# First rows of q through ScalarE's DMA queue, first rows of k through SyncE's

## The chip, the core and the metric

The kernel runs on one core of one Trainium2 chip. The metric is device time in microseconds, the median of several executions. The engines are named as in the profile: PE (TensorE), DVE (VectorE), ACT (ScalarE), POOL (GpSimd) and SP (SyncE); PEld is TensorE's weight load. SP, ACT and POOL can each issue DMA transfers through a queue of their own.

## The reference

Sliding-window causal attention (window 64) over q, k and v of shape 8 x 8 x 576 x 64 (batch, heads, positions, head dimension), and then a soft mixture of 8 experts with 4 slots each on the 4608 rows of 512 that come out:

```
scores = (q @ k^T) / 8, kept where 0 <= i - j < 64
attn   = softmax(scores);   x = attn @ v  ->  [4608, 512]
logits = x @ phi                              # 32 slots
d      = softmax over rows(logits);  slot_input = d^T @ x
slot_out[e] = relu(slot_input[e] @ w1[e]) @ w2[e]    # 8 experts
c      = softmax over slots(logits);  out = c @ slot_out
```

All inputs and the output are fp32 in device memory.

## The kernel before

The attention works on 32 pairs of heads, p = 0 to 31, four for each batch element. The order of all instructions is written out by hand; the loop at L553 interleaves the stages of several pairs, so that each engine executes its own instructions in the order of the text and waits where an operand is not there.

The rows of q and k are loaded in groups of four heads ("a quad"), two pairs. One partition holds six consecutive positions of a head, so a group is a tile of 96 partitions x 4 heads x 384 elements. `load_k` and `load_q` (L79) load groups 1 to 15 through POOL's queue, and these transfers turn fp32 into fp16 on their way. Group 0 is loaded otherwise, at L100 to L107: as fp32, without a cast, by four transfers of two heads (one pair) each, all issued by SP (L103) in the order k pair 0, q pair 0, k pair 1, q pair 1. They are put into memory that later holds the weights w1 of experts 5 and 4, which is why the profile calls them `w`. Each is 288 KB. `round_rows` (L110) then turns each into fp16, in tiles `ks` and `qs`: k pair 0 on ACT, q pair 0 on DVE, k pair 1 on DVE, q pair 1 on ACT.

From there: TensorE transposes the rows (`st_transpose`, L316, into PSUM tiles a_k and a_q); ACT or DVE copies them into `kT` (`st_copy_k`, L327 or L324) and `qb` (`st_copy_q`, L336, the second half of the first pair on DVE, L333). `st_max` (L346, L349) computes scores for the row maxima, which DVE reads at L353; `st_score` and `st_exp` (L372 to L381) compute them again for the exponentials; `st_av` (L405) multiplies with v; DVE normalises (L415). The transposed result goes through the slots' logits and a running soft dispatch (the `fr_` functions).

On ACT the first instructions are the load of the activation table and the copy into `lh` (L211), a constant of the masks. On DVE, constants are set before the cast of q pair 0 (L230), and the masks `wm` are copied (L233) between that cast and the cast of k pair 1 (L235). Behind that one stands the DVE half of `qb` (L333). After the four transfers SP issues one of phi (L254, 64 KB).

POOL's queue loads, after group 0, all of q, k and v, and the weights w1 and w2 of the experts as buffers come free (`load_w` L133 and L135, `load_half` L150 and L155). After the attention the experts are computed: `first` (L816), `turn_hidden` (L831), `second` (L837) and `second_last` (L846), the last of which uses the two tiles `w2h` that are loaded last. `osb` (L904, L910) takes the slots' outputs, half the columns each. `give` (L882) multiplies them with the combine weights, ACT and DVE scale the result in turn (L899, L897), and SP issues the output (L901): 14 transfers, the first three of the first half of the columns, the rest behind the second half.

Of the kernel before, what the change touches and what calls it, by code (L numbers as in the profile page):

```python
# [18 lines left out]
def kernel(  # L19
# [10 lines left out]
    nc = tc.nc  # L30
# [37 lines left out]
    RP = S // RQ  # L68
# [31 lines left out]
    for i, (src, tag, pr) in enumerate(((k, "ks", 0), (q, "qs", 0), (k, "ks", 1), (q, "qs", 1))):  # L100
        f = w1_t[5 - i // 2, 0][:, :, :].rearrange("p c f -> p (c f)").bitcast(FP32)
        f = f[0:RP, 768 * (i % 2):768 * (i % 2) + 768].rearrange("p (h x) -> p h x", h=2)
        nc.sync.dma_start(out=f, in_=src[0].rearrange("h (p r) d -> p h (r d)", p=RP)[:, 2 * pr:2 * pr + 2, :])  # L103
        if pr == 0:
            staged[tag] = pin.tile([128, 4, RQ * Dh], FP16, name=tag, tag=tag)
        first_rows[tag, pr] = f
        staged[tag, pr] = staged[tag], 2 * pr  # L107
# [569 lines left out]
    b, p = B - 1, NP - 1  # L677
# [273 lines left out]
```

## Time and profile before

| | |
|---|---|
| median of 3 runs | 191.47 us (191.35 to 192.05) |
| the profiled execution | 191.22 us |
| its span | 189.4 us |
| TensorE busy | 160.4 us (85%) |
| VectorE busy | 142.9 us (75%) |
| ScalarE busy | 144.9 us (76%) |
| GpSimd busy | 98.5 us (52%) |
| moved by DMA | 41.47 MB, mean 219 GB/s |
| of it GpSimd's queue (q0, software_dynamic) | 30.35 MB |
| of it SyncE's (q1, hardware_dynamic) | 10.68 MB |

The profiled execution has its own time, 191.22 us: the span of the trace and 1.8 us around it. All rows of the profile belong to that execution. A DMA row tells the issue (on the issuing engine's own row, as SPq) and, in the DMA view, the time from issue to landing. The share of a queue is the time that its packets took, added up over 16 DMA engines, and is over 100% where packets of an engine overlap. MB are counted as written, so a transfer that turns fp32 into fp16 reads twice as many.

### The profile page before, as it was taken

Reading aid. Unit: us, or ns where it says so; the run is one execution under the profiler, and the core shown is the slowest. Engines: PE = TensorE matmul, PEld = TensorE weight load, DVE = VectorE, ACT = ScalarE, POOL = GpSimd, SP = SyncE. Lnnn points to the kernel's source line nnn. Section 1 sums busy time; section 2 is a strip of 40 time slices with the busy share of each in tenths; the row PEclk is TensorE's granted clock in tenths of the full one; section 3 lists DMA queues with packets and bytes.
Section 4 is the critical chain, followed back from the end, with each engine's and each line's share of the span. In section 5 each row is a group of like instructions: output and inputs, shape, how many; then the busy total and the mean of one; then the engine's idle time right before and its main releaser. Section 6 shows DMA issues by size and latency. Waiting matters only on the chain. (4 is left out here: it accounts for less than half of the span.)

```text
span 189.4 us, 7060 instructions
## 1 busy us (share of the span) xinstructions
PE 160.4 (85%) x3036; PEld 120.5 (64%) x3036; DVE 142.9 (75%) x352; ACT 144.9 (76%) x266; POOL 98.5 (52%) x123
## 2 busy tenths in 40 slices
PE   5787999999999999999999899999989897769500
PEld 1466878877777777777777787776774365633100
DVE  6798796897888889788878988888886555289800
ACT  6487879989889898988999898988588256379600
POOL 7857927273695554983984828727854160000000
PEclk9999999999999999999999999999999999999955
DMA  6999999999999999999999999999999999979996
GB/s 153 222 184 185 226 175 223 179 223 179 185 226 180 210 192 184 207 196 185 210 195 192 211 182 198 199 204 195 213 214 212 204 196 179 277 258 422 415 415 252
DMA packets 61630, 41.47 MB, mean 219 GB/s; under 512 B 38816, under 2 KB 57504, under 8 KB 60704
## 3 DMA queue, kind: packets, MB, share of 16 engines
q0 software_dynamic: 56560, 30.35, 116.1%
q1 hardware_dynamic: 5040, 10.68, 15.9%
q8 instruction: 23, 0.38, 0.7%
q14 instruction: 7, 0.06, 0.1%
HBM read 61.93 MB, written 9.44 MB: 377 GB/s over the span
## 5 line engine op out<-in xcount | busy, mean ns | idle before, releaser
L336 ACT ACTIVATE qb<-a_q 64x576 f16<-64x576 f16 x63 | 40.6, 645 | 5.5 <-PE a_q L316 4.0
L353 DVE TENSOR_REDUCE m<-a_m 128x8 f16<-128x1024 f32 x32 | 39.2, 1224 | 1.0
L381 ACT ACTIVATE pt<-a_s 128x1024 f16<-128x1024 f32 x32 | 32.8, 1024 | 6.6 <-PE a_s L375 5.4
L180 POOL COPY v<-v 64x1152 f16<-64x1152 f16 x16 | 18.3, 1142 | 32.8 <-DMA v<-in_v_dram 32.6
L415 DVE TENSOR_TENSOR x_b<-a_v,rc 128x640 f16<-128x640 f32 x31 | 25.6, 825 | 1.1
L349 PEld LDWEIGHTS <-qb 128*128 128x128 f16 x256 | 16.8, 98 | 7.8 <-ACT qb L336 0.4
L346 PE MATMUL a_m<-wm,ident_h 128*128 128x512 f16 x64 | 19.3, 384 | 0.9 <-DVE m L353 0.9
L375 PEld LDWEIGHTS <-lh 128*128 128x128 f16 x288 | 18.8, 98 | 1.9 <-issue 1.7
L173 POOL DMA_DIRECT2D v<-in_v_dram x16 | 19.8, 1235 | 0.0
L372 PEld LDWEIGHTS <-kT 128*128 128x128 f16 x288 | 18.6, 98 | 1.6 <-issue 1.4
L372 PE MATMUL a_s<-qb,kT 128*128 128x128 f16 x256 | 19.5, 219 | 0.0
L349 PE MATMUL a_m<-kT,qb 128*128 128x128 f16 x256 | 19.5, 219 | 0.0
L375 PE MATMUL a_s<-rt,lh 128*128 128x128 f16 x256 | 19.5, 219 | 0.0
L433 ACT COPY xt<-a_k 128x576 f16<-128x576 f16 x28 | 17.9, 640 | 2.0 <-PE a_k L429 0.7
L182 POOL COPY v<-v 64x1088 f16<-64x1088 f16 (+1 forms) x16 | 17.9, 1120 | 0.8
L405 PE MATMUL a_v<-v,pt 128*64 128x65 f16 x558 | 15.6, 196 | 2.1 <-DVE m L363 1.1
L897 DVE TENSOR_SCALAR w<-cp,rcs 128x512 f32<-128x512 f32 (+1 forms) x22 | 12.9, 635 | 5.7 <-PE cp L892 5.4
L367 DVE CAST rt<-a_v 9x128 f16<-9x128 f32 x30 | 8.7, 289 | 11.0 <-PE a_v L366 10.7
L327 ACT ACTIVATE kT<-a_k 128x576 f16<-128x576 f16 x24 | 15.7, 654 | 0.8 <-PE a_k L316 0.8
L405 PEld LDWEIGHTS <-pt 128*64 128x64 f16 x576 | 13.5, 110 | 4.3 <-DVE m L363 1.8
L79 POOL DMA_DIRECT2D ks<-in_k_dram x15 | 10.4, 696 | 10.9 <-PE a_s L375 3.0
L316 PE MATMUL a_q<-ident_h,qs 96*64 96x96 f16 x384 | 14.7, 206 | 1.6 <-DVE a_q L225 1.3
(182 smaller groups left out, 332.6 us busy)
## 6 DMA issues: line engine op xcount, KB each, us to landing
w<-in_moe_w_dram POOLq DMA_DIRECT2D x13, 1024.0 KB, 16.8
out_dram<-w SPq DMA_DIRECT2D x9, 768.0 KB, 6.2
v<-in_v_dram POOLq DMA_DIRECT2D x16, 288.0 KB, 12.4
ks<-in_k_dram POOLq DMA_DIRECT2D x15, 288.0 KB, 15.2
qs<-in_q_dram POOLq DMA_DIRECT2D x15, 288.0 KB, 12.5
out_dram<-w SPq DMA_DIRECT2D x2, 640.0 KB, 4.4
w1h<-in_moe_w_dram POOLq DMA_DIRECT2D x4, 256.0 KB, 15.9
w<-in_moe_w_dram POOLq DMA_DIRECT2D x4, 256.0 KB, 14.8
```

The lines of the kernel that those rows point to most:

```text
L173: nc.gpsimd.dma_start(out=v1s[b % 2][:, c, 0:Dh], in_=v[b].rearrange("h s d -> (h s) d").rearrange("(c p) d -> p c d", p=128)[:, c, :])
L180: nc.gpsimd.tensor_copy(out=v2[64:128, c0:c1, 0:Dh], in_=v1[0:64, c0:c1, 0:Dh])
L182: nc.gpsimd.tensor_copy(out=v2[0:64, c0:c1, 0:Dh], in_=v1[64:128, c0 - 1:c1 - 1, 0:Dh])
L336: nc.scalar.activation(qbs[p % NQ][h, :, hf, :], turned(a_qh)[h], AF.Copy, scale=QKS)
L346: nc.tensor.matmul(a_m[:, j, :], ident_h[:, :], wm[:, j:j + 4, :].rearrange("p c x -> p (c x)"), start=True, stop=False, skip_group_check= ...
L349: nc.tensor.matmul(a_m[:, i // 4, 128 * (i % 4):128 * (i % 4) + 128], qblock(p, i), kwindow(p, i), start=False, stop=True, skip_group_chec ...
L353: nc.vector.reduce_max(ms[p % 2][:, 64:72].rearrange("p (l c) -> p l c", l=2), a_m[:, :, :].rearrange("p l (c x) -> p l c x", x=128), axis ...
L372: nc.tensor.matmul(at(i), kwindow(p, i), qblock(p, i), start=(i % 4 == 0), stop=False, skip_group_check=True)
L375: nc.tensor.matmul(at(i), lh[:, i, :], rt[:, :], start=False, stop=True, skip_group_check=True)
L381: nc.scalar.activation(st_pt(p)[:, 0:8, :].rearrange("p i x -> p (i x)"), a_s[:, :, :], AF.Exp, scale=XS)
L405: nc.tensor.matmul(a_v[r0:r0 + 64, hf, 65 * (i // 2):65 * (i // 2) + 65], pt[:, i, 64 * hf:64 * hf + 64], rhs, start=True, stop=True, skip ...
L415: nc.vector.tensor_tensor(out=xbs[b][:, :, 128 * hp:128 * hp + 128].rearrange("p c (l d) -> p l c d", l=2), in0=avv[:, :, :, 0:64], in1=rc ...
```

## The change

The two transfers of q (pair 0 and pair 1) are issued by ScalarE, the two of k by SyncE as before. The sizes, the destinations and the order in the text stay; everything else is unchanged.

```
     for i, (src, tag, pr) in enumerate(((k, "ks", 0), (q, "qs", 0), (k, "ks", 1), (q, "qs", 1))):
         f = w1_t[5 - i // 2, 0][:, :, :].rearrange("p c f -> p (c f)").bitcast(FP32)
         f = f[0:RP, 768 * (i % 2):768 * (i % 2) + 768].rearrange("p (h x) -> p h x", h=2)
-        nc.sync.dma_start(out=f, in_=src[0].rearrange("h (p r) d -> p h (r d)", p=RP)[:, 2 * pr:2 * pr + 2, :])
+        eng = nc.sync if tag == "ks" else nc.scalar
+        eng.dma_start(out=f, in_=src[0].rearrange("h (p r) d -> p h (r d)", p=RP)[:, 2 * pr:2 * pr + 2, :])
         if pr == 0:
             staged[tag] = pin.tile([128, 4, RQ * Dh], FP16, name=tag, tag=tag)
```

In ScalarE's order the two issues stand ahead of the table load and the copy into `lh`. In SyncE's order the issues of k pair 1 and of phi move up by one and by two places. The orders of TensorE, VectorE and GpSimd are the same as before. Lines after L102 have numbers higher by one in the changed kernel.

More of the change, by code (lines that the diff above doesn't have):

```diff
@@ L102 @@
         f = f[0:RP, 768 * (i % 2):768 * (i % 2) + 768].rearrange("p (h x) -> p h x", h=2)
-        nc.sync.dma_start(out=f, in_=src[0].rearrange("h (p r) d -> p h (r d)", p=RP)[:, 2 * pr:2 * pr + 2, :])
+        eng = nc.sync if tag == "ks" else nc.scalar
+        eng.dma_start(out=f, in_=src[0].rearrange("h (p r) d -> p h (r d)", p=RP)[:, 2 * pr:2 * pr + 2, :])
         if pr == 0:
```

## The prediction

> **What bounds the kernel now.** I read the page first, then the order of time in the first 20 us, the landing of each early transfer, the waits, and the last loads. Two stretches matter: the start, where the change is, and 163 us, where the last weights arrive.
>
> The start, in the timeline (start us, duration us, engine, line, operation, idle before and its releaser):
>
> ```profile
> 0.73 1.28 ACT L211 ACT_TABLE_LOAD   x1 [0.73 <-PEq L935]
> 1.17 0.44 SPq L103 DMA_DIRECT2D w<-in_q_dram  x1
> 2.16 1.15 ACT L211 COPY lh<-db 64x1152 f16<-64x1152 f16 x1
> 4.15 0.83 ACT L110 CAST ks<-w 96x768 f16<-96x768 f32 x1 [0.85 <-DMA w<-in_k_dram]
> 5.57 0.56 DVE L110 CAST qs<-w 96x768 f16<-96x768 f32 x1 [1.32 <-DMA w<-in_q_dram]
> 6.04 0.96 DVE L233 COPY wm<-wb 64x640 f16<-64x640 f16 x2
> 7.11 0.86 DVE L110 CAST ks<-w 96x768 f16<-96x768 f32 x1
> 8.01 0.76 DVE L333 TENSOR_SCALAR qb<-a_q 64x576 f16<-64x576 f16 x1
> 8.79 0.83 ACT L110 CAST qs<-w 96x768 f16<-96x768 f32 x1 [1.48 <-DMA w<-in_q_dram]
> 8.85 0.61 PE L349 MATMUL a_m<-kT,qb 128*128 128x128 f16 x8
> ```
>
> Call the four transfers k0, q0, k1, q1. The path to the first score maxima (L349 at 8.85) is VectorE's: it waits 1.32 us for q0, then runs the q0 cast, the mask copies, the k1 cast and its half of qb (L333) almost without a gap. ScalarE's part, kT done at 6.42 and its half of qb at 7.31, is early by 1.4 us or more.
>
> Landing of the four, from windows around each issue (the last number is us from issue to landing):
>
> ```profile
> w<-in_k_dram SPq DMA_DIRECT2D x1, 288.0 KB, 3.4
> w<-in_q_dram SPq DMA_DIRECT2D x1, 288.0 KB, 4.4
> w<-in_k_dram SPq DMA_DIRECT2D x1, 288.0 KB, 5.4
> w<-in_q_dram SPq DMA_DIRECT2D x1, 288.0 KB, 6.6
> ```
>
> Issued at 0.74, 1.17, 1.65 and 2.15, they land at 4.14, 5.57, 7.05 and 8.75: one each 1.45 to 1.7 us, although the issues are 0.45 us apart. So the transfers, not SyncE's issues, set the pace; k1 lands 0.06 us before VectorE is ready for it.
>
> How fast they run, in two half-microsecond windows of the DMA view (the first line from 4.5 us, the other three from 6.5; q1 is SyncE's queue, q0 GpSimd's, with packets, MB and share of 16 engines):
>
> ```profile
> DMA packets 74, 0.11 MB, mean 221 GB/s; under 512 B 2, under 2 KB 74, under 8 KB 74
> DMA packets 129, 0.12 MB, mean 241 GB/s; under 512 B 15, under 2 KB 129, under 8 KB 129
> q0 software_dynamic: 72, 0.06, 70.5%
> q1 hardware_dynamic: 57, 0.07, 51.3%
> ```
>
> At 4.5 us the only queue at work is SyncE's, with 74 packets in half a microsecond and a share near 98%. At 6.5 us GpSimd's queue (72 packets) works beside it (57), and together they finish 129. GpSimd's packets read fp32 and write fp16, so they are not the same load, but a second queue seems to fill engine time that one alone leaves.
>
> The end of the loads, in the waits (total us, times, longest):
>
> ```profile
> POOL v L180 <- DMA v<-in_v_dram: 32.6, 11, 4.7
> PE op L846 <- DMA w2h<-in_moe_w_dram: 0.8, 1, 0.8
> ```
>
> GpSimd's queue moves 1.86 to 2.09 MB in each 10 us from 20 to 160 us, landings there are 12 to 19 us after issue, and GpSimd itself waits for DMA. That stream is never empty. Its last w2h, issued at about 153.3, lands near 163.55; TensorE, ready at 162.97, waits for it until 163.75. Every full-width output comes after that matmul (L846). So time won by the computing engines at the start is held again there, and time lost is free up to 0.78 us. Only an earlier end of the load stream moves the end by itself.
>
> The sum is made against the profiled execution: 191.22 us, span 189.4 and 1.8 around it, 0.25 below the median of 191.47; the difference is applied to the median. A measurement of this kernel can tell about 0.5% (0.96 us) from no change.
>
> **SyncE.** Two issues go (0.44 and 0.45). k1 is issued at 1.17 instead of 1.65, phi at 1.65 instead of 2.64. phi landed at 10.9 and is first used at 26.6, so 0. The first outputs are issued from 160.49: 0.
>
> **ScalarE.** It now issues q0 and q1 ahead of the table load. On SyncE such an issue took 0.38 to 0.45, so I take 0.89 for two; bounds 0 (hidden beside the load) and 2.5 (two of GpSimd's longest, 1.26). Queued behind: the table load 1.62 to 2.90, the lh copy 2.90 to 4.05, then the k0 cast, which waited for DMA until 4.15. The 0.85 us of that wait just covers it. At 2.5 the cast begins at 5.7, kT ends at 8.0 and ScalarE's qb at 8.6, still ahead of L333's end at 8.77. So 0, as long as VectorE's chain stays where it is.
>
> **The transfers.** q0 is issued 0.44 earlier and q1 0.97, and each now runs beside a k transfer. Cost from both sides:
> - No overlap: both of a pair end when the second did, so k0 and q0 at about 5.57, k1 and q1 at about 8.6. k0 is covered. k1 is not: VectorE casts it at 8.6 instead of 7.11, L333 stands behind it, and TensorE's L349 behind that: +1.49.
> - Full overlap: 129 packets against 74 to 80, say 1.68 times the pace, so a pair takes 2.90/1.68 = 1.73. Counting 1.45 back from k0's landing gives 2.69 for a common origin: k0 and q0 at 4.42, k1 and q1 at 6.15. Then VectorE casts q0 at 4.42 to 4.98, copies the masks until about 6.05, casts k1 at 6.15 to 7.0 and ends L333 at about 7.8; L349 begins at 7.85, 1.0 earlier. The next k group, on GpSimd's queue, lands at 9.55 (issue 2.05 + 7.5; used at 10.21), and the next q group at 11.4 (2.88 + 8.5; used at 12.25), which caps the gain at 0.85.
>
> I take the second, as the window with two queues lies nearer to it: -0.85 for the computing engines. [...]
>
> **The load stream.** From 5 to 7 us SyncE's queue holds 95.5, 96.3, 81.7 and 51.3% of the engines by half microseconds, 1.62 us in all, while GpSimd's stream only begins (0.09 MB in 2 us, against 0.20 MB per us later). With full overlap the pairs are through at about 5.6, which leaves 1.0 us of engine time to the stream. Its first packets come at about 5.2 and rise slowly, so I take half: w2h 0.5 earlier. Against it, first outputs 0.85 earlier (57% of the engines' time from 160 to 165 was theirs) take from w2h's last packets, up to 0.4; I take 0.2. Net -0.3, bounds -1.0 and +0.4.
>
> Sum: TensorE ready at 162.1, w2h at 163.25, so the end moves by -0.3; 190.9 against the profiled execution, 191.2 as a median.
>
> **The rivals.**
> - *Pairs share the engines, no overlap.* One mechanism: k1 lands at 8.6 and VectorE's in-order queue holds L333 behind its cast. For it: the single queue's share is already 92 to 113%. Against it: 129 packets at 6.5 us. L349 +1.49, less the 0.78 that TensorE waits for w2h: +0.7, 192.2. It decides once k1 lands after 7.11 + 0.78 = 7.9. Bounds 0 (TensorE was only 81% busy from 10 to 20 us and may catch up) and +1.49 (192.95). [...]
> - *The stream moves with the start.* If GpSimd's first packets were held up by SyncE's, all of the 1.0 us comes back: w2h at 162.55, TensorE ready at 162.1, so -1.0, 190.5; bounds -0.8 and -1.5. Against it: the stream rose slowly, as if still being written.
> - *Nothing changes in kind.* The two queues are served one after the other, landings stay within 0.3 us: 191.5.
>
> **How the numbers follow.** Forecast 0.50, own range 190.6 to 191.9; pairs sharing 0.28; stream moving 0.17; nothing 0.05. Faster by over 0.5% (below 190.51): 0.13 of the stream case and 0.04 of the forecast's lower end, 0.17. Slower (above 192.43): 0.12 of the sharing case's upper part and 0.01 of the forecast, 0.13. The rest, 0.70, is within 0.5%. The range goes from 190.3 to 192.3.
>
> **What would show it.** Right: q0 lands at about 4.4 and k1 at about 6.2, L349 begins near 8.0, TensorE's wait for w2h at L846 grows from 0.78 to about 1.3, and GpSimd's queue has more than 0.09 MB by 7 us. Sharing is shown by k1 landing after 7.9, L349 after 9.6 and no wait at L846. The stream case shows in w2h landing by 162.7. The forecast is wrong if w2h lands where it did and the end still moves, or if ScalarE's two issues take so long that the k0 cast begins after 5.7.

## The result, and the profile after

| | before | changed kernel |
|---|---|---|
| median of 22 runs | 191.75 us (191.35 to 192.79) | 193.54 us (191.36 to 197.86) |
| the profiled execution, its span | 191.22, 189.4 us | 193.58, 191.8 us |

The changed kernel is slower. The ratio of the undisturbed runs is 1.0052, 95% interval 1.0033 to 1.007; it leaves out executions more than 1.5% above the fastest, of which the changed kernel had seven (195.0 to 197.9 us, whose timeline no run here shows), so it is smaller than that of the two medians, 1.0093. The forecast was 191.2 with a range to 192.3.

The start, in the timeline of the changed kernel (start us, duration us, engine, line, operation, idle before and its releaser; lines are one higher than before):

```profile
0.74 0.93 ACTq L104 DMA_DIRECT2D w<-in_q_dram  x2
1.70 1.28 ACT L212 ACT_TABLE_LOAD   x1 [1.70 <-PEq L936]
5.12 0.83 ACT L111 CAST ks<-w 96x768 f16<-96x768 f32 x1 [0.98 <-DMA w<-in_k_dram]
5.49 0.56 DVE L111 CAST qs<-w 96x768 f16<-96x768 f32 x1 [1.24 <-DMA w<-in_q_dram]
6.00 0.69 PE L317 MATMUL a_k<-ident_h,ks 96*64 96x96 f16 x12 [1.29 <-ACT ks L111]
7.03 0.86 DVE L111 CAST ks<-w 96x768 f16<-96x768 f32 x1
7.16 0.69 PE L317 MATMUL a_q<-ident_h,qs 96*64 96x96 f16 x12
8.45 0.82 ACT L111 CAST qs<-w 96x768 f16<-96x768 f32 x1
8.57 0.76 DVE L334 TENSOR_SCALAR qb<-a_q 64x576 f16<-64x576 f16 x1 [0.69 <-ACT qb L337]
10.20 1.06 PE L350 MATMUL a_m<-kT,qb 128*128 128x128 f16 x8
11.30 1.23 DVE L354 TENSOR_REDUCE m<-a_m 128x8 f16<-128x1024 f32 x1 [0.96 <-PE a_m L350]
```

Only k0 is later, by 0.97 us (cast at 5.12, before 4.15). q0 and k1 are cast 0.08 us earlier, and q1 no longer waits for DMA. But TensorE now stands idle for 1.29 us behind its warm-up matmuls, and what follows runs slowly: the transposes of q0 take 0.69 us and the eight matmuls of the first maxima 1.06, in the kernel before 0.45 and 0.61. The same rows of the kernel before, with TensorE idle for 0.33 us only:

```profile
5.03 0.69 PE L316 MATMUL a_k<-ident_h,ks 96*64 96x96 f16 x12 [0.33 <-ACT ks L110]
6.18 0.45 PE L316 MATMUL a_q<-ident_h,qs 96*64 96x96 f16 x12
9.80 1.22 DVE L353 TENSOR_REDUCE m<-a_m 128x8 f16<-128x1024 f32 x1
11.25 0.22 DVE L267 TENSOR_TENSOR lh<-lh,db 64x64 f16<-64x64 f16 x1
11.65 0.17 DVE L241 COPY rt<-ident_h 64x64 f16<-64x64 f16 x1
12.68 1.14 POOL L180 COPY v<-v 64x1152 f16<-64x1152 f16 x1
13.14 1.23 DVE L353 TENSOR_REDUCE m<-a_m 128x8 f16<-128x1024 f32 x1
```

The first read of maxima (L354, before L353) is 1.50 us late, the second 2.92 (16.06 against 13.14). What happens between them, in the changed kernel's timeline of VectorE and GpSimd:

```profile
12.39 1.14 POOL L181 COPY v<-v 64x1152 f16<-64x1152 f16 x1 [0.66 <-DMA v<-in_v_dram]
12.75 0.86 DVE L268 TENSOR_TENSOR lh<-lh,db 64x64 f16<-64x64 f16 x1
13.59 1.11 POOL L183 COPY v<-v 64x1088 f16<-64x1088 f16 x1
13.79 0.95 DVE L242 COPY rt<-ident_h 64x64 f16<-64x64 f16 x1
16.06 1.23 DVE L354 TENSOR_REDUCE m<-a_m 128x8 f16<-128x1024 f32 x1
```

Two small VectorE operations, 0.22 and 0.17 us before, take 0.86 and 0.95: both now run beside GpSimd's copies of v, and end within 0.1 us of them. In the kernel before, the last of these small operations ended at 11.91, ahead of the first copy at 12.68. That is another 1.42 us.

From the third read of maxima the lateness stays between 3.0 and 3.2 us; the first expert matmul (L817, before L816) is 3.17 late. Changed kernel, then before:

```profile
153.49 1.91 PE L817 MATMUL ha<-w,sit 128*32 128x512 f16 x32
150.32 1.91 PE L816 MATMUL ha<-w,sit 128*32 128x512 f16 x32
```

At the end, TensorE's wait for w2h is gone from the waits, and ScalarE waits less for the last slots' output (total us, times, longest; 2.5 before):

```profile
ACT qb L911 <- PE op L847: 1.6, 1, 1.6
```

The load stream did not move: the last two w2h are issued from 152.64, before from 152.51. Of the 3.17 us lost by the computing engines, 0.78 went into the wait that had been there, and 3.17 - 0.78 = 2.39 is the growth of the span, 189.4 to 191.8.

### The profile page after: what moved, and what is told of

Same layout as the page of the kernel before. It is cut to its first block, busy times and chain, and to the rows that moved or that the text cites. A ratio compares the mean times of both kernels' runs of the same rounds, so it can differ in the third digit from the quotient of the medians.

```text
span 191.8 us, 7060 instructions
## 1 busy us (share of the span) xinstructions
PE 162.2 (85%) x3036; PEld 121.0 (63%) x3036; DVE 145.1 (76%) x352; ACT 144.9 (76%) x266; POOL 98.5 (51%) x123
## 5 line engine op out<-in xcount | busy, mean ns | idle before, releaser
L354 DVE TENSOR_REDUCE m<-a_m 128x8 f16<-128x1024 f32 x32 | 39.2, 1224 | 1.9 <-PE a_m L350 1.0
L350 PEld LDWEIGHTS <-qb 128*128 128x128 f16 x256 | 17.3, 99 | 8.2 <-ACT qb L337 0.6
L347 PE MATMUL a_m<-wm,ident_h 128*128 128x512 f16 x64 | 19.8, 391 | 1.1 <-DVE m L354 1.1
L350 PE MATMUL a_m<-kT,qb 128*128 128x128 f16 x256 | 20.0, 222 | 0.1
L898 DVE TENSOR_SCALAR w<-cp,rcs 128x512 f32<-128x512 f32 (+1 forms) x22 | 12.9, 634 | 4.7 <-PE cp L893 4.5
L79 POOL DMA_DIRECT2D ks<-in_k_dram x15 | 10.4, 695 | 11.2 <-PE a_v L406 3.8
## 6 DMA issues: line engine op xcount, KB each, us to landing
qs<-in_q_dram POOLq DMA_DIRECT2D x15, 288.0 KB, 12.5
```

The lines of the kernel that those rows point to most:

```text
L347: nc.tensor.matmul(a_m[:, j, :], ident_h[:, :], wm[:, j:j + 4, :].rearrange("p c x -> p (c x)"), start=True, stop=False, skip_group_check= ...
L350: nc.tensor.matmul(a_m[:, i // 4, 128 * (i % 4):128 * (i % 4) + 128], qblock(p, i), kwindow(p, i), start=False, stop=True, skip_group_chec ...
L354: nc.vector.reduce_max(ms[p % 2][:, 64:72].rearrange("p (l c) -> p l c", l=2), a_m[:, :, :].rearrange("p l (c x) -> p l c x", x=128), axis ...
```

## The experiments

In all, the theory is that k0's late landing leaves TensorE idle and slow, and that what is late then meets GpSimd's copies. The rivals are lateness alone, the transfers at the end, and ScalarE's queue as such.

**More warm-up matmuls.** The changed kernel, with

```
-    warm_up(6)
+    warm_up(9)
```

> The changed kernel with nine warm-up matmuls before the first transposes instead of six. Theory clock: k pair 0 lands a microsecond later, TensorE stands idle for 1.29 us behind its warm-up and then runs at the slow pace (0.69 us for twelve transposes, 1.03 for two 512-column matmuls) until 11.4 us. Nine matmuls keep it busy from 1.96 to about 6.0; then L347 takes 0.60 again, L354 first runs before 10.2 (11.30 in the changed kernel, 9.80 in the one before), the copies of late_constants are out of the way of GpSimd's copies, and the time is 191.4 to 191.9. Rival, lateness: the 0.97 us of k pair 0 alone push the chain; the clock matters little, L354 first runs at 10.8 to 11.3 and the time stays at 193.0 to 193.6. Rival, transfers: the end is set by DMA, 193.5 whatever TensorE does.

191.81 us, median (12 runs), ratio 1.0028 (1.0007 to 1.0049). The kernel before had 191.69 beside it, so by the medians most of the loss is gone, though the interval leaves out 1. In the profiled execution k0 was almost as late, and at the first read that cost nothing:

```profile
1.96 3.60 PE L191 MATMUL a_m<-v 128*128 128x512 f16 x9 [1.96 <-DVE v L187]
5.03 0.83 ACT L111 CAST ks<-w 96x768 f16<-96x768 f32 x1 [0.90 <-DMA w<-in_k_dram]
6.61 0.45 PE L317 MATMUL a_q<-ident_h,qs 96*64 96x96 f16 x12
8.65 0.61 PE L350 MATMUL a_m<-kT,qb 128*128 128x128 f16 x8
9.60 1.23 DVE L354 TENSOR_REDUCE m<-a_m 128x8 f16<-128x1024 f32 x1
11.05 0.22 DVE L268 TENSOR_TENSOR lh<-lh,db 64x64 f16<-64x64 f16 x1
```

k0 is cast at 5.03, 0.88 later than in the kernel before, but TensorE is at its quick pace, the first maxima are read 0.20 earlier than before, and L268 is back at 0.22. So the lateness alone does not make the loss; slow matmuls are needed for it. The runs show two paces of TensorE, and no fixed limit at which one gives way to the other. Here it turned quick within its 3.60 us of warm-up (the last matmul took 0.38 us, the slow ones 0.63); in the changed kernel, after 2.74 us and a gap of 1.29, it stayed slow until 11.4. But with eight warm-up matmuls, 3.59 us without a gap, it was still slow at 5.49 (first kernel of the last experiment), and in the kernel with memsets behind, below, where the gap was 0.53, it was slow until 10.3:

```profile
5.49 0.69 PE L316 MATMUL a_k<-ident_h,ks 96*64 96x96 f16 x12
5.23 0.69 PE L319 MATMUL a_k<-ident_h,ks 96*64 96x96 f16 x12 [0.53 <-ACT ks L110]
```

The profile's row of the granted clock shows 9 in these slices all the same. So the pace is read from the durations alone, and what sets it was not shown; "clock", "cold" and "warm" in the expectations are the author's names for it. Three of the twelve runs still took 193.1 to 193.3, which stays open.

**The kernel before with fewer of them.**

```
-    warm_up(6)
+    warm_up(3)
```

> The kernel before with three warm-up matmuls instead of six; its four transfers stay on SyncE's queue. TensorE then stands idle for about 1.6 us ahead of the first transposes, which come at 5.03 as before. Theory clock: the transfers land as before (4.14, 5.57, 7.05, 8.75), but the matmuls run at the slow pace until 10 us or later, the first L353 moves from 9.80 to 10.4 to 10.9, and the time rises by 0.5 to 2.5 us, more if the copies of late_constants meet GpSimd's copies. Rivals, lateness and transfers: nothing lands later, so within 0.3 us of the kernel before.

191.63 us, 0.9998 (0.998 to 1.0016). The slow pace came, and the time did not follow; it stayed within 0.3 us, as the rivals had it. TensorE was idle for 1.61 us, the maxima's matmuls took 0.97 and the first read came at 10.28, 0.48 late, where 10.4 to 10.9 was expected:

```profile
5.03 0.69 PE L316 MATMUL a_k<-ident_h,ks 96*64 96x96 f16 x12 [1.61 <-ACT ks L110]
9.27 0.97 PE L349 MATMUL a_m<-kT,qb 128*128 128x128 f16 x8
10.28 1.23 DVE L353 TENSOR_REDUCE m<-a_m 128x8 f16<-128x1024 f32 x1 [0.73 <-PE a_m L349]
```

That kept VectorE's small operations (11.74 to 12.39) clear of GpSimd's copies but for the last (12.22), which stayed at 0.17. The first expert matmul was 0.46 late, and the wait for w2h shrank from 0.78 to 0.38:

```profile
PE op L846 <- DMA w2h<-in_moe_w_dram: 0.4, 1, 0.4
```

So at the first read the slow pace alone costs 0.48, the late k0 alone nothing (the run before), and both together 1.50. The traces show why the two do not simply add. In the kernel before, and in the changed one with nine warm-up matmuls, the first read comes as soon as VectorE has come through its own operations. At the slow pace TensorE works without a gap from the transposes of k0 to the maxima, 5.25 us here (5.03 to 10.28) and 5.30 in the changed kernel (6.00 to 11.30), and that is longer than VectorE's part; now TensorE's chain is the path, and the 0.97 us of k0 move all of it. Four other traces with the slow pace throughout have 5.15 to 5.30. VectorE's half of qb waits 0.69 us too in the changed kernel (L334), for ScalarE's half, but it ends at 9.33, ahead of the maxima at 10.20, so that wait costs nothing.

**VectorE's copies out of the way.** In the changed kernel:

```
+    make_rt(rts[0])          # ahead of it: NR, rts and make_rt
     round_rows("qs", 0, nc.vector.tensor_copy)
     ...
-            make_rt(rts[0])  # late_constants(1)
```

> The changed kernel with make_rt(rts[0]), three VectorE copies, moved from late_constants(1) to before the cast of q pair 0, into the 1.24 us in which VectorE waits for q. Theory collision: between the first and the second L354 the changed kernel loses another 1.4 us because two VectorE operations of 0.22 and 0.17 us take 0.86 and 0.95 beside GpSimd's copies of v (L181, L183). With the copies gone, only the addition to lh is left to meet them: the second L354 runs at 14.9 to 15.4 (16.06 in the changed kernel), and the time is 192.3 to 193.0; the first L354 stays at 11.3. Rival, everything is settled by the first L354: the second stays 2.9 us later than before and the time at 193.5. The cast of q pair 0 must not move by more than 0.2 us.

192.13 us, 1.002 (1.0006 to 1.0034), a little below the expected 192.3 to 193.0. The first read is at 11.32, the second at 14.98, in the expected window: the 2.92 us became 1.84. The first expert matmul is 1.72 late; less 0.78, 0.94 is left, and the span is 1.0 longer than before.

**Only q0 through ScalarE's queue.**

```
-        eng = nc.sync if tag == "ks" else nc.scalar
+        eng = nc.scalar if (tag, pr) == ("qs", 0) else nc.sync
```

> Only q pair 0 goes through ScalarE's queue; q pair 1 stays on SyncE's, behind k pair 1. Theory clock, with the two first transfers sharing the engines: k pair 0 still lands near 5.0 and q pair 0 near 5.4, TensorE is idle for over 1.1 us and cold until 11 us, and the time is that of the changed kernel within 0.5 us (193.0 to 194.0). Rival, ScalarE's second issue and the fourth transfer do the harm: k pair 0 lands at 4.2 to 4.5 and the time is 191.5 to 192.0.

193.26 us (191.43 to 197.37), 1.0076 (1.0046 to 1.0107), as expected. k0 is cast at 5.47, even later, though ScalarE issues one transfer only. The profiled execution was one of the quicker ones, 192.49: TensorE turned quick at 6.35 and slow again at 8.07, the first read came at 10.60, and the small operations just passed ahead of GpSimd's copy at 12.77. So TensorE's pace in these microseconds is not the same in each kernel with a late k0, and probably not in each execution: four of the changed kernel's 22 took 191.4 to 191.9 us, no longer than the kernel before, and no trace shows one of them.

**q behind the table load.** The changed kernel, with a one-element copy on ScalarE ahead of its two issues (the loop then issues k alone; the last line is cut short):

```
+    early = const.tile([128, 1], FP16, name="early")
+    nc.scalar.copy(out=early[64:128], in_=a_v[64:128, 0, 260:261])
+    for pr in range(2):
+        nc.scalar.dma_start(out=first_rows["qs", pr], ...)
```

> The changed kernel with a one-element copy on ScalarE ahead of its two transfers of q, so that the table load comes first and q pair 0 is issued at about 2.2 us instead of 0.74, when most of k pair 0 has gone through. If it is sharing the engines with q pair 0 that makes k pair 0 late, k pair 0 lands at 4.1 to 4.4 (5.04 in the changed kernel), TensorE is idle for 0.3 to 0.6 us and warm, the first maxima are read at 9.7 to 10.2, and the time is 191.4 to 191.9. Rival, ScalarE's queue does harm by itself (its sequencer, or two queues of this kind at a time): k pair 0 lands near 5 and the time is 193 or more.

191.12 us, 0.9985 (0.9961 to 1.0008): not told apart from the kernel before, and below the expected 191.4 to 191.9.

```profile
1.05 0.95 ACTq L120 DMA_DIRECT2D w<-in_q_dram  x2
4.02 0.83 ACT L111 CAST ks<-w 96x768 f16<-96x768 f32 x1 [0.67 <-DMA w<-in_k_dram]
5.29 0.57 DVE L111 CAST qs<-w 96x768 f16<-96x768 f32 x1 [1.06 <-DMA w<-in_q_dram]
9.58 1.23 DVE L359 TENSOR_REDUCE m<-a_m 128x8 f16<-128x1024 f32 x1
```

The issue did not wait for the end of the table load (0.73 to 2.01); it came at 1.05, only 0.31 us later than in the changed kernel, where 2.2 was expected. That was enough: k0 is cast at 4.02 and q0 at 5.29, each earlier than in the kernel before, and the first read is earlier than the expected 9.7 to 10.2. So neither ScalarE's queue nor the work of two queues is the harm, but that q0 starts at the same moment as k0.

**The queues crossed.**

```
-        eng = nc.sync if tag == "ks" else nc.scalar
+        eng = nc.scalar if tag == "ks" else nc.sync
```

> The changed kernel with the queues crossed: k through ScalarE's queue, q through SyncE's, all four issues at the same times. If two transfers that start together share the engines, whichever queue they are on, k pair 0 lands at 4.9 to 5.5 and the time is 192.5 to 194, as in the changed kernel. If ScalarE's queue is only served ahead of SyncE's, k pair 0 now lands near 4.1, q pair 0 late, and the time is 191.3 to 192.

193.56 us, 1.0077 (1.0042 to 1.0111). k0, now ScalarE's, is cast at 5.66, and q0, now SyncE's, at 5.26. Whichever queue has it, k0 is late when both start at 0.74; on ScalarE's it is later still.

**q0 first, in SyncE's queue alone.** The kernel before with the first two of the list swapped:

```
-((k, "ks", 0), (q, "qs", 0), (k, "ks", 1), (q, "qs", 1))
+((q, "qs", 0), (k, "ks", 0), (k, "ks", 1), (q, "qs", 1))
```

> The kernel before, all four on SyncE's queue, with q pair 0 ahead of k pair 0. k pair 0 then lands at about 5.57 without any second queue. Theory (late k pair 0, cold TensorE, collision): idle for about 1.7 us, slow matmuls until 11 us, the first maxima read at 11 or later, and 192.5 to 195. Rival, the second queue is what matters, not the order of landing: the time stays at 191.4 to 192.0.

193.46 us, 1.0047 (1.0006 to 1.0088). k0 is cast at 5.17, TensorE idle for 1.34 us, the first read at 11.20, the addition to lh 0.54 and one copy of rt 0.95 long: the changed kernel's picture with no second queue.

**The collision by itself.** The kernel before with four memsets on VectorE in late_constants(1), once ahead of the small operations, once behind them:

```
+            for i in range(4):
+                nc.vector.memset(idle, 1.0)      # ahead: here
             nc.vector.tensor_tensor(out=lh[64:128, 0, 0:64], ...)
             make_rt(rts[0])                      # behind: after this line
```

> The kernel before with four memsets of 128 x 320 (about 1.2 us of VectorE) put ahead of the addition to lh and make_rt in late_constants(1); the first maxima stay at 9.80. Theory collision: the small operations now run at 12.4 and later, beside GpSimd's copies of v (12.7 to 15.0), and two of them take 0.8 us or more instead of 0.2. The second read of maxima moves from 13.14 by 1.2 for the memsets and by 1 to 1.6 for the collision, to 15.3 to 16.0, and the time to 192.8 to 193.6. Rival, what is late is only pushed: 14.2 to 14.5, and 191.8 to 192.2. The next kernel has the same memsets behind the small operations.

> The same four memsets behind make_rt in late_constants(1) instead of ahead of it: the same work on VectorE, but the small operations run at 11.2 to 11.9 as before, clear of GpSimd's copies. Theory collision: the second read of maxima at 14.1 to 14.5, later stages 1.0 to 1.3 us late, 0.78 of it hidden by the wait for w2h, 191.6 to 192.2. Rival: the same as with the memsets ahead.

195.95 and 195.46 us (four runs each). The times can't be set against each other: in the second kernel's profiled execution TensorE was slow and in the first one's it was not, though up to the first read both have the same order of instructions as the kernel before, and the memsets took 1.70 us, not 1.2. The expected 191.6 to 192.2 of the second was a miss; 192.8 to 193.6 of the first also. The stage itself can be compared. Ahead, then behind:

```profile
9.58 1.23 DVE L356 TENSOR_REDUCE m<-a_m 128x8 f16<-128x1024 f32 x1
12.88 1.17 DVE L241 COPY rt<-db 64x128 f16<-64x128 f16 x1
14.07 1.07 DVE L242 COPY rt<-ident_h 64x64 f16<-64x64 f16 x1
16.45 1.23 DVE L356 TENSOR_REDUCE m<-a_m 128x8 f16<-128x1024 f32 x1
```

```profile
10.53 1.22 DVE L356 TENSOR_REDUCE m<-a_m 128x8 f16<-128x1024 f32 x1 [0.87 <-PE a_m L352]
12.13 0.22 DVE L241 COPY rt<-db 64x128 f16<-64x128 f16 x1
12.36 0.17 DVE L242 COPY rt<-ident_h 64x64 f16<-64x64 f16 x1
15.57 1.23 DVE L356 TENSOR_REDUCE m<-a_m 128x8 f16<-128x1024 f32 x1
```

From first to second read it is 6.87 us against 5.04, and 5.04 is the kernel before's 3.34 plus 1.70. The difference of 1.83 is that of the two copies, 0.95 and 0.90, which ran beside GpSimd's copies of v (12.79 to 15.11). Each ends with one of them: the copy that begins at 12.88 lasts until 14.05, and GpSimd's first ends at 13.97; the one that begins at 14.07 lasts until 15.14, and GpSimd's second ends at 15.11. Why they do was not shown.

**Both guards.** Eight warm-up matmuls and make_rt moved up, in the kernel before and in the kernel with q behind the table load:

> The kernel before with eight warm-up matmuls and make_rt(rts[0]) ahead of the cast of q pair 0; the four transfers stay on SyncE's queue. Theory: the cold stretch and the collision can then not come in any execution, so the spread between executions shrinks (191.0 to 192.8 in the kernel before), but the median is held by the last w2h: 191.2 to 191.6. Rival, the computing engines set the end: as the second read of maxima comes 0.3 to 0.6 us earlier, 190.8 to 191.1.

> q through ScalarE's queue behind the table load, as in the run that issued it there, with eight warm-up matmuls and make_rt(rts[0]) ahead of the cast of q pair 0. Theory: maxima read at 9.6 and 12.5 to 12.9 in every execution, TensorE waits for w2h again, 190.6 to 191.2 and a spread under 1 us. Rival, the gain of that run was chance: 191.3 to 191.8, no better than the kernel before with the same guards.

The first: 191.67 us, 0.9987 (0.9963 to 1.0011), and a spread of 1.5 us (190.81 to 192.34 in 12 runs), against 2.1 for the kernel before beside it (190.95 to 193.09 in 29). In its profiled execution the transposes of k0 and q0 were still slow (0.69 and 0.56), k1 and q1 landed later (casts at 7.66 and 9.43), and the first read was at 10.28. So eight warm-up matmuls do not rule out the slow stretch. The second: 191.23 us (190.04 to 192.72), 0.9976 (0.9946 to 1.0006), first read at 9.20, second at 12.22, 0.92 earlier than before. The computing engines are 0.5 us ahead at the first expert matmul (149.85), and TensorE waits for w2h again:

```profile
PE op L852 <- DMA w2h<-in_moe_w_dram: 0.7, 1, 0.7
```

The lowest medians are those of the two kernels with q behind the table load, but neither is faster than the kernel before beyond its interval. Both expectations missed, if narrowly for the medians: the spread of the first shrank little if at all, that of the second was 2.7 us where under 1 was expected, and its reads came earlier than the expected 9.6 and 12.5 to 12.9.

## Why the prediction was wrong

Two steps failed: the pace of two queues, from which the forecast -0.85 at the first read came, and that a late k0 is covered, through which +1.50 came instead.

- **The step on which the forecast stood: full overlap.** It let k0 and q0 land at 4.42 and k1 at 6.15. k0 and q0 landed at 5.0 and 5.4, k1 at about 7.0, as before. By 5.0 us, 553 packets had passed in the two queues, against 548 in the one. The window with 129 packets was the wrong row: there the second queue was GpSimd's. The no-overlap bound did not come either: k1 was not at 8.6. After 5 us there may be some gain, as q1 landed at about 7.8 instead of 8.75, but in the runs with one queue it lands anywhere from 7.8 to 9.4.
- **The step that made the loss: k0 is covered.** At the no-overlap bound the working let k0 land at 5.57 and called it free, as ScalarE's part of the path had 1.4 us to spare. It counted operations at the durations that the trace had, and missed that TensorE would run slowly for microseconds after the longer gap: from 6.00 to 11.4, after 1.29 us. It also missed order: q0's transposes stand behind k0's on TensorE, so q0, though on time, was transposed 0.98 later. At the slow pace TensorE's own chain, 5.30 us from k0's transposes to the first read, is the path, and k0's 0.97 counts in full: +1.50 at the first read. And the spare time was read too wide: in the traces where VectorE waits ahead of its half of qb, that half begins as ScalarE's ends (8.57 and 8.54 in the changed kernel), so ScalarE's end at 7.31 was early for VectorE's start at 8.01 by 0.7, not 1.4.
- **A term that was missing.** The prediction moved VectorE's small operations in time and did not ask what would run beside them there: +1.42.
- **ScalarE's issues.** 0.89 us was forecast, 0.93 came, and the k0 cast still waited 0.98 for DMA: right.
- **The load stream.** 0.5 earlier was forecast; the last two w2h are issued 0.13 later, and GpSimd's queue had moved 0.05 MB by 7 us, not more than 0.09. What was read from the stream held: the wait for w2h absorbed 0.78 of the lateness in the changed kernel and with VectorE's copies out of the way, and 0.40 of 0.46 with three warm-up matmuls.
- **A slip in the sum.** The gain was capped at 0.85 by the next q group; the next k group, landing at 9.55 and used at 10.21, would by the same reckoning have capped it at 0.66. It changes nothing here, as no gain came.
- **The slower rival** had the sign but not the mechanism: k1 was to hold VectorE. That its +1.49 at L349 is near the +1.35 measured there (10.20 against 8.85) is chance.

Open: what decides in an execution whether TensorE is slow in these microseconds, and why two queues that start together moved fewer packets at first.

## What to carry to other kernels

A transfer that starts a chain can be late if another starts beside it at the same moment, even on a queue of its own: k0 was cast at 5.12 instead of 4.15, and it was enough to issue it 0.3 us ahead of q0. Before a late operand is called covered, ask what idles meanwhile and at which pace it comes back, which engine's chain is then the path, and where the small operations that stand behind it will land. The trace of before had a sign of each: its first twelve transposes took 0.69 us and the next 0.45, and one copy of 64x128 (L240, at 15.26) took 0.92 us instead of 0.22, beside a DMA issue of GpSimd. And look for a wait at the far end, as 0.78 us here, which decides how much of a loss is seen.

## What the runs showed of the hardware

- ScalarE's DMA issues did not wait for the operations ahead of them in its order: with a table load and a copy ahead, they came at 1.05, while the load ran from 0.73 to 2.01 and the copy came at 2.02. With nothing ahead of them, the table load came after both issues, at 1.70.
- With two queues that start together fewer packets passed at first: by 3.0 us 125 in the changed kernel, 220 in the one before; by 5.0 us they were level (553 and 548). In the four other runs with such a start it was 115 to 141 by 3.0 us, in the other runs with one queue 175 to 207. With q issued 0.31 us later it was 184 and 198, and by 5.0 us 607 and 655.
- A VectorE copy of 64 x 64 elements took 0.17 us in the kernel before (11.65), with no GpSimd copy beside it, and in the changed kernel 0.95 and 1.17 (13.79 and 18.45) beside GpSimd copies that began at 13.59 and 18.44.
- A VectorE copy was also longer beside a DMA issue of GpSimd: that of 64x128 at 15.26 in the kernel before took 0.92 instead of 0.22 and lasted until 16.18, and GpSimd's issue of v ran from 14.92 to 16.15. Not each one was: in the changed kernel one of 64x64 took 0.17 at 14.66, as GpSimd's issue of v began. The rows of the first:

```profile
15.26 0.92 DVE L240 COPY rt<-db 64x128 f16<-64x128 f16 x1
14.92 1.23 POOL L173 DMA_DIRECT2D v<-in_v_dram  x1
```
